# ScalarE's queue around the copy of a pair's second keys: attention, two MoE layers, one core

## The chip, the core and the metric

The kernel runs on one NeuronCore of a Trainium2 chip. The core's engines work side by side, each through a queue of its own in order: TensorE (PE: matrix products and transposes into PSUM; PEld is its weight load), VectorE (DVE), ScalarE (ACT), GpSimd (POOL) and SyncE (SP, which here issues DMAs). The metric is the device time of one execution in microseconds (us). The time before is 1155.35 us, the median of 3 runs (1152.71 to 1155.36).

## The reference

What is computed, cut to what matters (4 batches, 12 heads, 448 tokens, head size 64):

```
def _attn_ref(q, k, v, g_q, g_k):
    q_n, k_n = (rmsnorm(q, g_q), rmsnorm(k, g_k))
    scores = np.matmul(q_n, k_n.transpose(0, 1, 3, 2)) / np.sqrt(64)
    scores = scores - np.max(scores, axis=-1, keepdims=True)
    attn = np.exp(scores)
    return np.matmul(attn / (attn.sum(-1, keepdims=True) + 1e-09), v)
x = attention.transpose(0, 2, 1, 3).reshape(1792, 768)
h = np.maximum(x @ w_in, 0.0);  x = (h * h) @ w_out     # 768 -> 2048 -> 768
return (((x @ w1) * (x @ w2)) @ w3) @ moe2_w_out         # 768 -> 1024 -> 1024 -> 768
```

Products are made from a high and a low part of each operand (three matmuls for one product), so that every weight and every intermediate tile is split: a rounded copy (the high part) and the difference (the low part).

## The kernel before

The program is one loop over the 48 heads `h`, with one extra turn, and a generator of matmuls of the MoE layers that the loop draws on. `fill(n)` takes some n matmuls from it. While batch b's heads run (heads 12 to 23 are the second batch), the generator works on the MoE layers of an earlier batch: heads 0 to 12 have a product of weights (`gen_w3o`) beside them, 13 to 24 the MoE layers of the first batch (with the 64-bit weights that have to be turned into float32: `words` on ACT and POOL, `join` on DVE), 25 to 48 those of the second and part of the third. The rest follows behind the loop.

Heads go in pairs, an even one and the odd one behind it. The query rows of a pair are cut into seven chunks of 128: `CHUNKS` gives chunks 0 to 3 to the even head, 4 to 6 to the odd one, and chunk 3 holds the last 64 rows of both. So the scores of chunk 3, which the even head's turn makes, need the keys of the odd head. From head 12 on (`early`, line 1182) the keys of the next, odd head are therefore transposed in the even head's turn: `stage_k(h + 1)` (line 1185) issues four PE transposes (line 941) into the one PSUM bank `kv`, and ACT copies them to SBUF as the tile `kt` (line 943, shown as L144, the line of the helper). `stage_qk(h, 1)` behind it issues the scores (lines 956 and 957) of chunks 2 and 3; those of chunk 3 read the new `kt`. In this text "odd head 19" stands for the place in head 18's turn where the keys of head 19 are copied and used.

What stands in ACT's queue in such a turn, by the names in the rows: `vt` (copy out of the `kv` bank at the end of the head before), `vhl` (high part of v, `v_prep`), `nb` (line 988, scaling of the negated row maxima that DVE reduces in line 967), `p` (line 991, the exponentials), `ptr` and `pte` (high part of the transposed probabilities), `hl` (high part of a weight, `split_hi`), `raw` (lines 333 and 337, `words`), `r`, `act`, `acc`, `x`, `osb` (evictions of the MoE layers), `qn` and `nt` (statistics of the norm, every fourth head).

The order in each queue is not the order of the code. A scheduler takes what is ready first by its own estimate, and the code's order decides between equals. `issue_after(ins)` adds an edge without a semaphore: what is traced inside of it on `ins`'s engine stands behind `ins` in the queue. Before the change only `load` moves and the first heads use it. From the last half of the last batch's MoE layers on the order is the written one (`in_order`).

Of the kernel before, what the change touches and what calls it, by code (L numbers as in the profile page):

```python
# [8 lines left out]
F32 = mybir.dt.float32  # L9
# [21 lines left out]
def attention_moe_kernel(  # L31
# [18 lines left out]
    S = P * C  # L50
# [3 lines left out]
    NH = B * H  # L54
# [87 lines left out]
    def copy_on(eng, out, in_):  # L142
        if eng == "a":
            return nc.scalar.activation(out=out, in_=in_, func=AF.Copy)  # L144
        if eng == "g":
            return nc.gpsimd.tensor_scalar(out=out, in0=in_, scalar1=1.0, scalar2=1.0, op0=ALU.mult, op1=ALU.mult)
        return nc.vector.tensor_copy(out=out, in_=in_)
# [665 lines left out]
    def load_head(h):  # L813
        if not (0 <= h < NH):
            return
        b, hh = divmod(h, H)
        t = t2.tile([128, S], F32, name="qt", tag="qt")
        nc.sync.dma_start(out=t, in_=q_t[b, hh])
        qts[h] = t

    def load_v(h):
        if not (0 <= h < NH):
            return
        b, hh = divmod(h, H)
        t = t2.tile([128, C, D], F32, name="v", tag="v")
        nc.sync.dma_start(out=t, in_=v_in[b, hh])
        vs[h] = t
# [106 lines left out]
    def stage_k(h):  # L934
        if not (0 <= h < NH):
            return
        d = heads[h]
        khl = d.pop("khl")
        ps = ps_kv.tile([128, 512], F32R, name="kv", tag="kv")
        for c in range(C):  # L940
            nc.tensor.transpose(ps[:, c * P:(c + 1) * P], khl[:, c, :], ident_r[:P, :P])
        kt = t2.tile([128, S], F32R, name="kt", tag="kt")
        copy_on("a", kt, ps[:, :S].bitcast(F32))
        d["kt"] = kt

    def stage_qk(h, s):
        if not (0 <= h < NH):
            return
        d = heads[h]
        nb = d["nb"] = small.tile([128, 2], F32, name="nb", tag="nb")  # L950
        chunks = CHUNKS[h % 2][s]
        n = len(chunks)
        o = d["sc"] = [None] * n

        def score(out, d, at, m):
            nc.tensor.matmul(out, d["qh"][:, at:at + m], d["kt"], start=True, stop=False)  # L956
            nc.tensor.matmul(out, d["ql"][:, at:at + m], d["kt"], start=False, stop=True)  # L957

        for j, c in enumerate(chunks):
            ps = ps_sc.tile([128, 512], F32, name="sc", tag="sc")  # L960
            o[j] = ps[:, :S]
            if c == 3:
                score(o[j], heads[h + 1], S - 128, 128)
                score(o[j][:MIX], d, S - MIX, MIX)
            else:
                score(o[j], d, (c % 4) * 128, 128)
            nc.vector.tensor_reduce(out=nb[:, j:j + 1], in_=o[j], axis=AX.X, op=ALU.max, negate=True)  # L967
        if h < H:
            nc.vector.tensor_tensor(  # L969
                out=nb[:, :n], in0=nb[:, :n], in1=d["rq"][:, chunks[0]:chunks[0] + n], op=ALU.mult  # L970
            )
# [36 lines left out]
    def stage_words(h, s):  # L1008
        if not (H <= h < NH):
            return  # L1010
        d = heads[h]
        chunks = CHUNKS[h % 2][s]
        n = len(chunks)
        words = t3.tile([128, 2, S], F32R, name="pw", tag="pw")
        nc.sync.dma_start(out=words[:, :n].bitcast(F32), in_=d.pop("pp")[:, :n])
        for j, c in enumerate(chunks):
            d["p"][c] = words[:, j, :]

    def stage_sums(h):
        if 0 <= h < NH and h % 2:  # L1020
            flat, turned = sums2[h // 2]
            for b in range(0, 128, 32):
                nc.sync.dma_start(out=flat[:, b:b + 32], in_=turned[b:b + QC])
            sums2[h // 2] = flat
# [35 lines left out]
    def stage_lo(h):  # L1060
        if not (0 <= h < NH):
            return
        d = heads[h]
        for lo, p, hi in d["lo"]:
            sub_on("v", lo, p, hi)
        d["lo"] = []
# [51 lines left out]
    def fill(n):  # L1118
        state["credit"] += n
        while state["gen"] is not None and state["credit"] > 0:  # L1120
            try:
                k = next(state["gen"])
                state["credit"] -= k
                state["left"] -= k
            except StopIteration:
                state["gen"] = None
# [29 lines left out]
    for h in range(NH + 1):  # L1156
        n = W3O / ((H + 1) * 6) if h <= H else (MOE / (H * 6) if h <= 2 * H else (MOE + IN) / (2 * H * 6))
        late = h > 2 * H
        if h < 2:
            load_head(h + 3)  # L1160
            load_v(h + 1)
        if not late and h % GH == 0:
            load_group(h // GH + 1)
        stage_qk(h, 0)
        fill(n)
        if h <= 2 * H + 1:
            stage_sums(h - 1)
        stage_exp(h, 0)
        if h > 2 * H:
            stage_words(h, 0)  # L1170
        if h == 0:
            group_prep(0, "rest")
        if h >= 2:
            load_head(h + 3)
            load_v(h + 1)
        if late and h % GH == GH - 1:
            load_group((h + 1) // GH + 1)
        if h % H != 1:
            stage_x(h - 2)
        stage_t(h - 1, 0)  # L1180
        stage_t(h - 1, 1)
        early = H <= h and h % 2 == 0
        fill(n)
        if early:
            stage_k(h + 1)
        stage_lo(h - 1)
        if h < NH:
            v_prep(h)
        fill(n)
        if h <= 2 * H:  # L1190
            stage_words(h, 0)
        stage_rows(h - 1)
        even = H <= h
        if even:
            stage_qk(h, 1)
        if not early:
            stage_k(h + 1)
        stage_t(h - 1, 2)
        stage_t(h - 1, 3)
        fill(n)  # L1200
        stage_lo(h - 1)
        if not even:
            stage_qk(h, 1)
            fill(n)
        stage_exp(h, 1)
        if h > 2 * H:
            stage_words(h, 1)
        fill(n)
        if even:
            fill(n)  # L1210
        if h <= 2 * H:
            stage_words(h, 1)
        stage_v(h - 1)
        if h >= 2 * H and h % GH < 2:
            group_prep(h // GH + 1, "qk"[h % GH])
        elif h % GH == 1:
            group_prep(h // GH + 1)
        head_prep(h + 2)
        if h and h % H == 0:
            if h != 3 * H:  # L1220
                fill(1e9)
            stage_x(h - 1)
            if h == H:
                start_fill(gen_moe(0), MOE)
            elif h == 2 * H:
                in_order(SP)
                start_fill(gen_late(), MOE + IN)
            elif h == NH:
                start_fill(gen_pair(), MOE)
# [61 lines left out]
```

## Time and profile before

| | |
|---|---|
| time, median of 3 runs | 1155.35 us |
| profiled execution, its own time | 1159.42 us |
| span of the profile, first to last instruction | 1157.6 us |
| PE busy | 1124.8 us, 97% |
| DVE / ACT / POOL busy | 790.3 / 776.6 / 608.9 us |
| share of the chain that ended last | PE 67%, ACT 12%, DMA 7%, DVE 7% |

The profile's page gives the busy time of each engine, the span in 40 slices, the DMA queues, the chain of waits that ended last and the costliest groups of instructions. A name such as `sc<-kt` is a tile written and a tile read. A duration is that of one instruction; instructions of one engine overlap a little, so that the distance from start to start is shorter than the duration. Times are in us from the start of the span.

### The profile page before, as it was taken

The page shows a single profiled execution, that of the slowest core. Times are in us where ns is not written, and L with a number is a line of the kernel's source. Part 1 is how long each engine was busy: PE and PEld are TensorE (multiplying, and loading weights), DVE is VectorE, ACT ScalarE, POOL GpSimd, SP SyncE. Part 2 cuts the span into 40 slices and gives each one's busy share as a digit, 9 for nine tenths or more (in the row PEclk, how much of TensorE's full clock was granted, in tenths as well). Part 3 has the DMA queues.
Part 4 walks back from the last instruction along what each step waited for, and adds up shares of the span by engine and source line. Part 5 has one row for each costly group of instructions (what it writes and reads, how often), then busy time and mean ns, then how long its engine had stood idle before and what let it go on. Part 6 is the DMA issues. An engine that isn't in the chain of part 4 may idle for free.

```text
span 1157.6 us, 18785 instructions
## 1 busy us (share of the span) xinstructions
PE 1124.8 (97%) x5958; PEld 1019.5 (88%) x5958; DVE 790.3 (68%) x1363; ACT 776.6 (67%) x1768; POOL 608.9 (53%) x609
## 2 busy tenths in 40 slices
PE   7789999999999999999999999999999999999998
PEld 4678888999889899989989899999999899999997
DVE  6889888878898854565674755564544315887886
ACT  6889978888878866767776666776764435533352
POOL 3375433445545455957876776684865854011131
PEclk8899999999999999999999999999999999999999
DMA  7867757898998863565655657665556664243423
GB/s 237 264 201 211 235 160 243 306 297 293 321 294 276 279 190 120 165 213 178 219 172 163 207 182 236 197 197 165 171 170 202 215 193 126 69 135 105 130 83 123
DMA packets 130899, 229.74 MB, mean 198 GB/s; under 512 B 17472, under 2 KB 84544, under 8 KB 130800
## 3 DMA queue, kind: packets, MB, share of 16 engines
q1 hardware_dynamic: 129072, 225.79, 61.3%
q10 hardware_dynamic: 1728, 2.75, 0.7%
q8 instruction: 47, 0.77, 0.3%
q14 instruction: 52, 0.43, 0.1%
HBM read 162.53 MB, written 37.05 MB: 172 GB/s over the span
## 4 chain that ended last, share of the span: by engine, by line
PE 67%; ACT 12%; DMA 7%; DVE 7%; issue 3%; POOL 1%; SPq 1%; DVEq 0%; ACTq 0%; POOLq 0%
PE mm L411 16%; PE mm L412 16%; PE mm L413 16%; PE kv L1091 4%; PE pt L1045 3%; PE sc L956 2%; ACT p L991 2%; PE sc L957 2%; ACT raw L333 2%; ACT hl L144 2%; DMA raw<-wo 1%; DVE raw L346 1%; ACT ptr L144 1%; DMA raw<-w_in 1%; DMA raw<-w_out 1%
## 5 line engine op out<-in xcount | busy, mean ns | idle before, releaser
L150 POOL TENSOR_TENSOR hl<-raw,hl 128x384 fp32r<-128x384 f32 (+1 forms) x286 | 333.1, 1171 | 289.6 <-ACT hl L144 245.7
L144 ACT ACTIVATE hl<-raw 128x384 fp32r<-128x384 f32 (+1 forms) x405 | 227.8, 566 | 152.5 <-PE mm L413 40.1
L411 PE MATMUL mm<-x,hl 128*128 128x448 f32 (+1 forms) x640 | 238.3, 372 | 1.2 <-ACT x L144 1.2
L412 PE MATMUL mm<-x,hl 128*128 128x448 f32 (+1 forms) x640 | 234.2, 366 | 0.8 <-DVE x L150 0.8
L413 PE MATMUL mm<-x,hl 128*128 128x448 f32 (+1 forms) x640 | 233.7, 365 | 0.2 <-DVE hl L150 0.2
L411 PE MATMUL mm<-act,hl 128*128 128x448 f32 (+1 forms) x544 | 201.6, 371 | 1.9 <-ACT act L144 1.9
L412 PE MATMUL mm<-act,hl 128*128 128x448 f32 (+1 forms) x544 | 198.8, 365 | 3.7 <-DVE act L150 2.0
L413 PE MATMUL mm<-act,hl 128*128 128x448 f32 (+1 forms) x544 | 197.9, 364 | 0.1
L967 DVE TENSOR_REDUCE nb<-sc 128x1 f32<-128x448 f32 x168 | 102.6, 615 | 73.8 <-PE sc L957 72.4
L411 PEld LDWEIGHTS mm<-x,hl 128*128 128x128 f32 x640 | 121.0, 189 | 10.9 <-ACT x L144 2.3
L412 PEld LDWEIGHTS mm<-x,hl 128*128 128x128 f32 x640 | 121.0, 189 | 10.4 <-DVE x L150 1.8
L413 PEld LDWEIGHTS mm<-x,hl 128*128 128x128 f32 x640 | 120.9, 189 | 9.8 <-DVE hl L150 0.5
L991 ACT ACTIVATE p<-sc,nb,rr 128x448 f32<-128x448 f32 x168 | 121.3, 723 | 11.5 <-DVE nb L969 8.8
L150 DVE TENSOR_TENSOR ptr<-pt,ptr 128x512 fp32r<-128x512 f32 (+1 forms) x144 | 85.9, 617 | 57.9 <-ACT ptr L144 57.4
L412 PEld LDWEIGHTS mm<-act,hl 128*128 128x128 f32 x544 | 102.8, 189 | 12.3 <-DVE act L150 3.0
L411 PEld LDWEIGHTS mm<-act,hl 128*128 128x128 f32 x544 | 102.8, 189 | 9.5 <-ACT act L144 2.3
L413 PEld LDWEIGHTS mm<-act,hl 128*128 128x128 f32 x544 | 102.8, 189 | 8.0 <-DVE hl L150 0.4
L339 POOL TENSOR_SCALAR raw<-raw 128x384 uint32<-128x384 uint16 (+1 forms) x80 | 57.2, 716 | 83.1 <-DMA raw<-w_out 20.7
L346 DVE SCALAR_TENSOR_TENSOR raw<-raw 128x384 uint32<-128x384 uint32 (+1 forms) x120 | 86.4, 728 | 18.5 <-POOL raw L339 9.6
L956 PE MATMUL sc<-kt,qh 128*128 128x448 f32 (+1 forms) x192 | 74.8, 389 | 14.3 <-ACT p L991 7.4
L150 DVE TENSOR_TENSOR hl<-raw,hl 128x384 fp32r<-128x384 f32 (+1 forms) x119 | 80.0, 675 | 7.9 <-ACT hl L144 7.8
L333 ACT ACTIVATE raw<-raw 128x384 f32<-128x384 f32 (+1 forms) x120 | 71.6, 601 | 15.6 <-DMA raw<-w_in 7.7
(153 smaller groups left out, 2122.0 us busy)
## 6 DMA issues: line engine op xcount, KB each, us to landing
pw<-p SPq DMA_DIRECT2D x54, 448.0 KB
raw<-f_in SPq DMA_DIRECT2D x96, 192.0 KB
raw<-f_out SPq DMA_DIRECT2D x72, 256.0 KB
raw<-w_in SPq DMA_DIRECT2D x32, 384.0 KB
raw<-w_out SPq DMA_DIRECT2D x24, 512.0 KB
raw<-w SPq DMA_DIRECT2D x32, 384.0 KB
qt<-q_t SPq DMA_DIRECT2D x48, 224.0 KB
raw<-f SPq DMA_DIRECT2D x56, 192.0 KB
```

Of the source, the lines that this page charges most:

```text
L144: return nc.scalar.activation(out=out, in_=in_, func=AF.Copy)
L150: return (nc.vector if eng == "v" else nc.gpsimd).tensor_tensor(out=out, in0=in0, in1=in1, op=op)
L333: nc.scalar.activation(out=hi, in_=hi, func=AF.Prelu, scale=2.0**-112, alpha=-(2.0**32))
L339: nc.gpsimd.tensor_scalar(out=t[:, :n, 0], in0=low, scalar1=2.0**-13, scalar2=2.0**-14 - 0.5, op0=ALU.mult, op1=ALU.add)
L346: nc.vector.scalar_tensor_tensor(out=f[:, :n].bitcast(U32), in0=t[:, :n, 1], scalar=3, in1=t[:, :n, 0], op0=ALU.logical_shift_left, op1=AL ...
L411: nc.tensor.matmul(ps, w[:, 0, wk, :], x[0], start=(i == 0), stop=False)
L412: nc.tensor.matmul(ps, w[:, 0, wk, :], x[1], start=False, stop=False)
L413: nc.tensor.matmul(ps, w[:, 1, wk, :], x[0], start=False, stop=(i == last))
L956: nc.tensor.matmul(out, d["qh"][:, at:at + m], d["kt"], start=True, stop=False)
L967: nc.vector.tensor_reduce(out=nb[:, j:j + 1], in_=o[j], axis=AX.X, op=ALU.max, negate=True)
L991: nc.scalar.activation(out=p, in_=o[j], func=AF.Exp, scale=d["rq"][:, c:c + 1], bias=nb[:, j:j + 1], accum_out=sm[:, c:c + 1],)
L1091: nc.tensor.matmul(ps[:, :S], w, m, start=(n == 0), stop=(n == len(ops) - 1))
```

## The change

`stage_k` returns the instruction of the copy to `kt`. In the turns of even heads from 12 on, what is traced between `stage_k(h + 1)` and the end of the next `fill(n)` is placed behind that copy on ACT. In that stretch stand `stage_lo` (no work of ACT), `v_prep` (one copy on ACT) and the part of the MoE layers that `fill` draws (splits, words, evictions).

```
@@ -940,8 +940,8 @@
         kt = t2.tile([128, S], F32R, name="kt", tag="kt")
-        copy_on("a", kt, ps[:, :S].bitcast(F32))
         d["kt"] = kt
+        return copy_on("a", kt, ps[:, :S].bitcast(F32)).ins
@@ -1181,12 +1181,14 @@
         early = H <= h and h % 2 == 0
         fill(n)
-        if early:
-            stage_k(h + 1)
+        ahead = ExitStack()
+        if early and h + 1 < NH:
+            ahead.enter_context(tc.issue_after(stage_k(h + 1)))
         stage_lo(h - 1)
         if h < NH:
             v_prep(h)
         fill(n)
+        ahead.close()
```

No instruction is added or removed; the scheduler places them anew. From head 25 on, ACT's queue differs at each odd head by the copy `vhl`, which moves from well ahead of the copy `kt` to behind it. At odd head 37 (both pieces are of ACT's queue, the first in the turn's first third, the second at the copy):

```order
 L837 ACTIVATE nt<-nt 128x32
 L144 ACTIVATE vt<-kv 64x448
-L144 ACTIVATE vhl<-v 128x4x64
 L838 ACTIVATE nt<-nt 128x32
 L988 ACTIVATE nb<-nb,rr 128x1
...
 L144 ACTIVATE hl<-raw 128x384 x2
 L144 ACTIVATE kt<-kv 128x448
+L144 ACTIVATE vhl<-v 128x4x64
 L144 ACTIVATE act<-gf 128x448
 L144 ACTIVATE hl<-raw 128x384
```

Only `vhl` has moved; everything between the two pieces reads alike in both.

In the second batch more moves: words go behind `kt` too, and other instructions change places on ACT, DVE and POOL. At odd head 19 ACT's queue stood so before:

```order
L333 ACTIVATE raw_3814<-raw_3814 128x512
L144 ACTIVATE vt<-kv 64x448
L144 ACTIVATE vhl<-v 128x4x64
L483 ACTIVATE r<-mm 128x448
L144 ACTIVATE hl<-raw 128x512
L486 ACTIVATE act<-r 128x448
L988 ACTIVATE nb<-nb,rr 128x1 x2
L991 ACTIVATE p,sm<-sc,nb,rr 128x448 x2
L144 ACTIVATE ptr<-pt 128x384 x2
L144 ACTIVATE hl<-raw 128x512
L483 ACTIVATE r<-mm 128x448
L144 ACTIVATE kt<-kv 128x448
```

and from `nb` on it stands so now (`vt` is the row ahead of these, and `act`, `vhl` and `raw_3814` are the rows behind):

```order
L988 ACTIVATE nb<-nb,rr 128x1
L483 ACTIVATE r<-mm 128x448
L144 ACTIVATE hl<-raw 128x512
L486 ACTIVATE act<-r 128x448
L991 ACTIVATE p,sm<-sc,nb,rr 128x448
L988 ACTIVATE nb<-nb,rr 128x1
L144 ACTIVATE ptr<-pt 128x384
L991 ACTIVATE p,sm<-sc,nb,rr 128x448
L144 ACTIVATE ptr<-pt 128x384
L144 ACTIVATE hl<-raw 128x512
L483 ACTIVATE r<-mm 128x448
L144 ACTIVATE kt<-kv 128x448
```

The word `raw_3814` and `vhl` have left; the same eleven instructions stand ahead of `kt`, but the first `nb` now leads them. On DVE the join of `raw_3814`, which stood between the join of `raw_3743` and `xf`, has gone behind the low part of `vhl` as well.

At odd head 23, DVE's queue around the row maxima `nb` stood so before (`raw` rows are joins, `xf` the addition that empties the `kv` bank):

```order
L346 SCALAR_TENSOR_TENSOR raw<-raw_4888 128x384
L967 TENSOR_REDUCE nb<-sc 128x1
L1099 TENSOR_TENSOR xf<-kv,vt 64x448
L967 TENSOR_REDUCE nb<-sc 128x1
L542 TENSOR_TENSOR mm<-mm,r 128x448
```

and so now:

```order
L346 SCALAR_TENSOR_TENSOR raw<-raw_4869 128x384
L346 SCALAR_TENSOR_TENSOR raw<-raw_4888 128x384
L1099 TENSOR_TENSOR xf<-kv,vt 64x448
L967 TENSOR_REDUCE nb<-sc 128x1 x2
L542 TENSOR_TENSOR mm<-mm,r 128x448
```

The first reduction has moved behind `xf`; the joins ahead of it are the same.

## Rows read from the trace of the kernel before

**Rows 1.** Busy time by stretch; length, engines, PEclk, DMA share, GB/s

```profile
205.00:400.00 195.00, 191.01 (x1022) 173.96 (x1021) 170.44 (x292) 163.52 (x391) 95.88 (x103) 0.99 0.88 293
400.00:850.00 450.00, 446.72 (x2437) 408.54 (x2436) 255.84 (x414) 312.18 (x734) 308.93 (x292) 1.00 0.59 188
```

**Rows 2.** PE's waits, 205 to 850 us: total, times, longest

```profile
PE sc L956 <- ACT kt L144: 6.6, 6, 1.8
PE pt L1045 <- DVE ptr L150: 0.3, 1, 0.3
PE kv L941 <- DVE xf L1099: 0.2, 1, 0.2
```

**Rows 3.** PE timeline at odd heads 19 to 37: start, us, [idle before]

```profile
294.87 0.47 PE L956 MATMUL sc<-kt,qh 128*128 128x448 f32 x1 [1.51 <-ACT kt L144]
339.81 0.47 PE L956 MATMUL sc<-kt,qh 128*128 128x448 f32 x1 [0.35 <-ACT kt L144]
...
380.76 0.37 PE L957 MATMUL sc<-kt,ql 128*128 128x448 f32 x1
382.88 0.47 PE L956 MATMUL sc<-kt,qh 128*128 128x448 f32 x1 [1.75 <-ACT kt L144]
383.19 0.37 PE L957 MATMUL sc<-kt,ql 128*128 128x448 f32 x1
383.39 0.36 PE L956 MATMUL sc<-kt,qh 128*64 128x448 f32 x1
...
513.07 0.47 PE L956 MATMUL sc<-kt,qh 128*128 128x448 f32 x1 [1.48 <-ACT kt L144]
586.53 0.47 PE L956 MATMUL sc<-kt,qh 128*128 128x448 f32 x1 [0.92 <-ACT kt L144]
659.34 0.47 PE L956 MATMUL sc<-kt,qh 128*128 128x448 f32 x1 [0.58 <-ACT kt L144]
```

**Rows 4.** Busy time by stretch, 380 to 390 us (columns as in rows 1)

```profile
380.00:390.00 10.00, 8.25 (x37) 7.06 (x36) 8.50 (x16) 9.19 (x24) 4.73 (x6) 0.83 0.90 312
```

**Rows 5.** ACT timeline at odd heads 37 and 33

```profile
653.83 0.40 ACT L144 ACTIVATE vhl<-v 128x256 fp32r<-128x256 f32 x1
654.14 0.21 ACT L838 ACTIVATE nt<-nt 128x32 f32<-128x32 f32 x1
...
580.38 0.23 ACT L837 ACTIVATE nt<-nt 128x32 f32<-128x32 f32 x1 [2.69 <-DVE nt L836]
```

**Rows 6.** DVE and ACT timeline at odd head 29

```profile
507.52 0.62 DVE L967 TENSOR_REDUCE nb<-sc 128x1 f32<-128x448 f32 x1
...
507.85 0.40 ACT L144 ACTIVATE vhl<-v 128x256 fp32r<-128x256 f32 x1
508.18 0.29 ACT L988 ACTIVATE nb<-nb,rr 128x1 f32<-128x1 f32 x1
```

**Rows 7.** ACT timeline at odd head 21

```profile
333.70 0.29 ACT L988 ACTIVATE nb<-nb,rr 128x1 f32<-128x1 f32 x1 [0.62 <-DVE nb L967]
...
339.21 0.54 ACT L144 ACTIVATE kt<-kv 128x448 fp32r<-128x448 f32 x1
```

**Rows 8.** DVE, then ACT timeline at odd head 19

```profile
288.65 0.69 DVE L346 SCALAR_TENSOR_TENSOR raw<-raw 128x512 uint32<-128x512 uint32 x1 [0.54 <-POOL raw L339]
289.79 1.14 DVE L967 TENSOR_REDUCE nb<-sc 128x1 f32<-128x448 f32 x2
...
289.14 0.54 ACT L483 ACTIVATE r<-mm 128x448 f32<-128x448 f32 x1
294.25 0.56 ACT L144 ACTIVATE kt<-kv 128x448 fp32r<-128x448 f32 x1
```

**Rows 9.** ACT timeline at odd head 23

```profile
376.63 0.29 ACT L988 ACTIVATE nb<-nb,rr 128x1 f32<-128x1 f32 x1 [1.88 <-DVE nb L967]
381.82 0.57 ACT L333 ACTIVATE raw<-raw 128x384 f32<-128x384 f32 x1
382.26 0.56 ACT L144 ACTIVATE kt<-kv 128x448 fp32r<-128x448 f32 x1
```

More of the change, by code (lines that the diff above doesn't have):

```diff
@@ L942, in stage_k @@
         kt = t2.tile([128, S], F32R, name="kt", tag="kt")
-        copy_on("a", kt, ps[:, :S].bitcast(F32))
         d["kt"] = kt
+        return copy_on("a", kt, ps[:, :S].bitcast(F32)).ins
     def stage_qk(h, s):
@@ L1183, in attention_moe_kernel @@
         fill(n)
-        if early:
-            stage_k(h + 1)
+        ahead = ExitStack()
+        if early and h + 1 < NH:
+            ahead.enter_context(tc.issue_after(stage_k(h + 1)))
         stage_lo(h - 1)
@@ L1189, in attention_moe_kernel @@
         fill(n)
+        ahead.close()
         if h <= 2 * H:
```

## The prediction

> **What bounds the kernel now.** I read the busy times by stretch first, because the change acts only between the first odd head it touches and the end of the loop. There the reader sees a PE that is busy for 191.0 of 195 us and 446.7 of 450 us, at a granted clock of 0.99 and 1.00 of full speed, while ACT is busy for 163.5 and 312.2 us [rows 1]. PE sets the time; another engine matters only where PE waits for it. Who that is, the view of waits says: between 205 and 850 us PE sits idle for 6.6 us, in six places, for the copy `kt`, and for 0.5 us for anything else; it waits for no weight, no eviction and no transfer [rows 2]. The timeline of PE then shows the six places: the odd heads 19, 21, 23, 29, 33 and 37, with 1.51, 0.35, 1.75, 1.48, 0.92 and 0.58 us of idle time [rows 3]. The twelve other odd heads that the change touches lose almost nothing.
>
> A place costs a little more than its idle time. At head 23 the scores start at 380.76, then at 382.88 and, one matmul later, at 383.19 [rows 3]. Undisturbed, such matmuls follow each other every 0.20 us (383.19 to 383.39). So 2.12 + 0.31 - 0.40 = 2.03 us are lost for 1.75 us of idle time, 0.28 more. With 0.28 for each of the six the waits cost 6.6 + 1.7 = 8.3 us.
>
> Behind the longest wait the clock falls: between 380 and 390 us the mean granted clock is 0.83 of full speed [rows 4], which is 10 x 0.17 / 0.5 = 3.4 us at the lower of the two levels, 1.2 GHz. Work in it takes twice as long, so 1.7 us are lost. No other wait of rows 3 has that behind it: the stretch from 400 to 850 us, with three of them, has a clock of 1.00 [rows 1]. Together 10.0 us is all that this change can win at `kt`, 0.9% of the time.
>
> **What the change takes away, from head 25 on.** The copy `kt` is late because ACT has a backlog: at head 23 it starts at 382.26 straight behind a word that started at 381.82, with no pause between them [rows 9]. What can make it earlier is what leaves the queue ahead of it. From head 25 on that is `vhl` alone, one copy of 0.40 us, 12 times (front part, first order rows). Three of these places have a wait.
> - Head 37: `vhl` starts at 653.83 and the next instruction at 654.14, so 0.31 us leave [rows 5]. ACT works without a pause from there to `kt`. The wait of 0.58 us becomes 0.27.
> - Head 33: behind `vhl` ACT sits idle for 2.69 us until 580.38, for the statistics on DVE [rows 5]. What leaves ahead of that only makes the pause longer: nothing is won, 0.92 us stay.
> - Head 29: `nb` starts at 508.18, right behind `vhl`. But it also needs DVE's reduction, which runs from 507.52 for 0.62 us, to 508.14 [rows 6]. Without `vhl` it starts at the same moment: nothing is won, 1.48 us stay.
>
> **What it does in the second batch** (heads 13 to 23). Here words leave as well, but other instructions change places, so I count ACT's queue from `nb` to `kt` anew.
> - Head 21: from `nb` at 333.70 to `kt` at 339.21 are 5.51 us [rows 7]. Three words leave, of 0.44 us each (as at head 23, 381.82 to 382.26 [rows 9]). One other word, one weight split and one short `nt` come in between, 0.44 + 0.5 + 0.2 as I estimate from the distances around them. That is 5.51 - 1.32 + 1.14 = 5.3 us. `nb` itself can come earlier, since the maxima now stand ahead of the norm's statistics on DVE. So `kt` starts by 339.0 at the latest, ends 0.54 us later, and the wait of 0.35 us shrinks to 0.1 or goes; I take it as gone, with its surcharge 0.6 us.
> - Head 19: before, `r` starts at 289.14 and `kt` at 294.25; eleven instructions in 5.11 us [rows 8]. The same eleven stand there now, but led by `nb`, which waits for DVE. On DVE the join at 288.65 leaves (0.69 us and 0.54 us of waiting ahead of it), so that the first reduction starts about 1.2 us before 289.79, at 288.6, and ends 0.6 us later [rows 6, 8]. 289.2 + 5.1 = 294.3: `kt` is where it was, and 1.5 us of idle time stay. What was won at the words is lost because `r`, `hl` and `act`, which ran while DVE was at work, now stand behind `nb`.
> - Head 23: from `nb` at 376.63 to `kt` at 382.26 are 5.63 us [rows 9]. The word at 381.82 (0.44 us) leaves and another comes; a split of about 0.5 us moves ahead of `nb`. That makes about 5.1 us. But `nb` now comes later: DVE's first reduction stands behind `xf`, one instruction of about 0.5 us. The two cancel, and 1.75 us and the fall of the clock stay.
> - Heads 13, 15 and 17 have no wait to lose. I take 0 for them; the third case below prices the other side.
>
> **What is moved behind.** `vhl` is read at the end of the next turn, and the words that move are taken up three units ahead of use; DVE's and POOL's parts of them stand later in their queues too, so they do not block. That PE waits for no weight and no `vhl` now [rows 2] says there is cover; 0 is my value. If the cover failed, each of the twelve words that move could cost its own 0.57 us [rows 9] at the weight that it feeds: 6.8 us is the other end, and only a slower DVE or transfer chain could bring a part of it.
>
> **The sum.** 0.31 + 0.6 = 0.9 us off the profiled execution: 1159.42 - 0.9 = 1158.5 us. That execution ran 4.07 us over the median of the runs (1155.35), and the waits should be in both; so I forecast 1155.35 - 0.9 = 1154.4 us. This is under 0.3% (3.5 us), which is about what a measurement of this kernel can tell from no change.
>
> **The rivals.**
> - *The waits of the second batch go.* For it speaks that words of 0.44 us leave at every one of its places, and that at head 19 ACT could start the eleven instructions at once behind `vt` if DVE came earlier by more than the 1.2 us I count. Against it: at 19 and 23 my count puts `kt` where it was. Price: at 19 1.51 + 0.28, at 23 1.75 + 0.28, and the 1.7 us of the clock with it, on top of 0.9: 6.4 us, 1149.0 us. If 29 and 33 went too, 3.0 us more; but nothing leaves the queue there that binds.
> - *The clock alone.* The Trainium skill, page "TensorE: Matmul & The Clock Gate", section "What's actually happening", says that a gate sets the array's clock by how busy the engine has been of late. By that rule a shorter wait at head 23 would give back the slow stretch too. The trace bears it out as far as the fall follows the longest wait, and does not settle it, since 1.51 and 1.48 us had none behind them. In rows: a wait that shrinks at 23 from 1.75 to 1.4 us wins 0.35 + 1.7, on top of 0.9: 1152.4 us. I count this with the first half of the range.
> - *`nb` ahead of work that was ready makes `kt` later* (slower). In the second batch the scheduler now puts `nb`, which waits for DVE, in front of `r`, `hl` and `act`. If DVE's first reduction at head 19 is not earlier than before, it ends at 290.4, and `kt` starts at 290.4 + 5.1 = 295.5, 1.25 us later. It decides from the point where that reduction ends after 289.15. Were it so at 19 and 23, and at two of 13, 15 and 17 for about 0.8 us each, it is 2.5 + 1.6 = 4.1 us, and each wait that grows past 1.75 us may bring 1.7 us of slow clock, taken once: 5.8 us less the 0.9 won, 1160.2 us. For it speaks the order at 19; against it that the joins ahead of the maxima on DVE get fewer.
> - *The change does not do what it says.* From head 25 on it nearly does not: the splits and evictions ahead of `kt` were traced ahead of it and stay. This is in my forecast.
>
> **How the numbers follow.** The forecast 0.52 (its own range 1152.5 to 1156.5), the first rival 0.14, the clock 0.12, the slower one 0.17, and 0.05 for a gain at 29 and 33 beside those. The first rival and the last lie below 1151.9 us (0.3%), and a fifth of the clock's and the forecast's spread reaches there too: faster 0.23. The slower rival lies half beyond 1158.8 us as it stands or with a second fall of the clock, and some spread comes on top: slower 0.14. The rest, 0.63, is within 0.3%. The range that holds 8 in 10 takes in the first rival, from 1148.8, and ends short of the slower one's full price, at 1158.8; a gain at 29 and 33 and the failed cover are left out.
>
> **What would show it.** In the changed kernel's view of PE's waits for `kt` between 205 and 850 us: the idle time of six places should fall from 6.6 to about 5.9 us, with head 37 near 0.27 us, 29 and 33 at 1.5 and 0.9, 21 gone, 19 and 23 near 1.5 and 1.75. No wait of PE for weights or `vhl` should appear. I am wrong if 19 and 23 are gone or if a wait stands at 13, 15 or 17; if the waits are as I say and the time still moves by over 3 us, the clock or the part behind 850 us did it.

## The result, and the profile after

The changed kernel takes 1159.14 us (median of 15 runs), the kernel before 1154.41 us in the same comparison (15 runs): a ratio of 1.0065, 95% interval 1.0049 to 1.0081. This ratio is the comparison's estimate over all runs of both kernels; the quotient of the two medians is 1.0041 (4.7 us), that of the means 1.0059. The forecast was 1154.4 us and no measurable change; the kernel became slower, by an amount just past the end of the range.

| | before | after |
|---|---|---|
| profiled execution, its own time, us | 1159.42 | 1163.71 |
| TensorE busy, 205 to 400 us | 191.01 | 187.56 |
| TensorE busy, 400 to 850 us | 446.72 | 446.96 |
| its waits for `kt`, 205 to 850 us | 6.6 us, 6 times | 5.6 us, 4 times |
| its waits for the transfer `pw` there | under 0.2 us | 2.9 us, 3 times |

The first view to read is again the busy time by stretch, with the columns of [rows 1]; here of the changed kernel:

```profile
205.00:400.00 195.00, 187.56 (x998) 170.90 (x996) 169.87 (x288) 159.32 (x376) 89.07 (x98) 0.99 0.87 286
400.00:850.00 450.00, 446.96 (x2444) 409.83 (x2445) 264.73 (x418) 315.65 (x742) 310.01 (x293) 1.00 0.60 190
```

Against [rows 1], TensorE loses 3.45 us of busy time and 24 matmuls in the second batch, and gains 0.24 us behind it. The loss is in the part where the forecast expected a gain of 0.6. TensorE's waits in the changed kernel, 205 to 850 us (total, times, longest):

```profile
PE sc L956 <- ACT kt L144: 5.6, 4, 2.4
PE pt L1045 <- DMA pw<-p: 2.9, 3, 2.1
PE pt L1045 <- DVE ptr L150: 1.2, 2, 0.6
PE kv L941 <- DVE xf L1099: 0.4, 1, 0.4
```

The waits for `kt` fall by 1.0 us against [rows 2], as meant. What is new is the second line: the transposes of the probabilities wait for `pw`, the transfer on SP's queue that turns the exponentials `p` into the tile the transposes read. Two of its three places (the third wait is 0.3 us, at 400 us) and those of `kt`, on TensorE's timeline (start, duration, idle before); at 361.83, between them, the transposes wait for DVE's low part `ptr`:

```profile
221.80 0.71 PE L1045 MATMUL pt<-ident_r,pw 128*128 128x128 f32 x6 [0.53 <-DMA pw<-p]
...
294.43 0.47 PE L956 MATMUL sc<-kt,qh 128*128 128x448 f32 x1 [2.37 <-ACT kt L144]
...
361.83 0.37 PE L1045 MATMUL pt<-ident_r,pw 128*128 128x128 f32 x2 [0.59 <-DVE ptr L150]
...
375.32 0.28 PE L1045 MATMUL pt<-ident_r,pw 128*128 128x128 f32 x2
377.73 0.45 PE L1045 MATMUL pt<-ident_r,pw 128*128 128x128 f32 x3 [2.13 <-DMA pw<-p]
...
385.71 0.47 PE L956 MATMUL sc<-kt,qh 128*128 128x448 f32 x1 [1.14 <-ACT kt L144]
...
515.18 0.47 PE L956 MATMUL sc<-kt,qh 128*128 128x448 f32 x1 [1.53 <-ACT kt L144]
587.83 0.47 PE L956 MATMUL sc<-kt,qh 128*128 128x448 f32 x1 [0.52 <-ACT kt L144]
```

Against [rows 3]: heads 21 and 37 have no wait left, 29 is unchanged, 19 has grown from 1.51 to 2.37 us, and a wait of 2.13 us stands at 377.73, where there was none. The clock falls once, as before, but now behind head 19 instead of head 23 (compare [rows 4]):

```profile
290.00:300.00 10.00, 7.55 (x33) 6.15 (x32) 7.79 (x15) 10.00 (x25) 5.47 (x6) 0.83 0.88 272
380.00:390.00 10.00, 8.86 (x50) 7.76 (x49) 7.16 (x15) 9.47 (x25) 4.05 (x5) 1.00 0.96 292
```

**Why `pw` is late at 377.73.** SP's queue of the changed kernel (SPq rows: start, time to issue, line; L319 loads a raw weight, L354 stores a joined one):

```profile
356.26 0.50 SPq L354 DMA_DIRECT2D f<-raw  x1
363.04 0.33 SPq L319 DMA_DIRECT2D raw<-w  x1
363.41 0.43 SPq L354 DMA_DIRECT2D f<-raw  x1
363.94 0.49 SPq L1015 DMA_DIRECT2D pw<-p  x1
...
369.03 0.94 SPq L354 DMA_DIRECT2D f<-raw  x1
372.31 0.33 SPq L319 DMA_DIRECT2D raw<-w  x1
372.69 0.42 SPq L354 DMA_DIRECT2D f<-raw  x1
373.21 0.47 SPq L1015 DMA_DIRECT2D pw<-p  x1
```

SP stands still from 356.8 to 363.0 and from 370.0 to 372.3, each time at a load, and `pw` is issued behind it: the second one at 373.21, against 366.67 before, and TensorE asks for it at 375.60. The load waits for a buffer, which a join on DVE sets free:

```profile
SPq L319 <- DVE raw L346: 12.7, 7, 5.4
```

This is SP's wait for joins between 335 and 375 us; it was 7.3 us in all, 4.1 the longest, before. The join itself ends at 363.01, just ahead of the load at 363.04; ACT's timeline at its word, and DVE's at the join:

```profile
361.41 0.57 ACT L333 ACTIVATE raw<-raw 128x384 f32<-128x384 f32 x1
361.85 0.58 ACT L337 ACTIVATE raw<-raw 128x384 uint32<-128x384 uint16 x1
...
361.08 1.29 DVE L150 TENSOR_TENSOR ptr<-pt,ptr 128x512 fp32r<-128x512 f32 x2 [0.57 <-ACT ptr L144]
362.45 0.56 DVE L346 SCALAR_TENSOR_TENSOR raw<-raw 128x384 uint32<-128x384 uint32 x1
```

The join now stands behind two low parts and starts when the second piece of its word has ended (362.43), because this word (`raw_4650`) was moved from between the exponentials to behind the copies `ptr` on ACT: 361.41 instead of 354.68, 6.7 us later, where its neighbours are about 2.2 us later. SP's own order at this place is the same in both kernels.

**The two profiled executions.** Their times differ by 4.3 us, but not by these waits alone. Taking the same matmul in both traces: the changed kernel is 2.2 us ahead at 170 us, 1.7 behind at 432, 0.3 behind at 849, and 4.3 behind at the end. The last 4 us are the last 220 us of the program, where no wait differs; experiment 7 is on that.

### The profile page after: what moved, and what is told of

It is laid out like the page before. It is cut to its first block, busy times and chain, and to the rows that moved or that the text cites. A ratio compares the mean times of both kernels' runs of the same rounds, so it can differ in the third digit from the quotient of the medians.

```text
span 1161.9 us, 18791 instructions
## 1 busy us (share of the span) xinstructions
PE 1124.4 (97%) x5958; PEld 1016.9 (88%) x5958; DVE 801.8 (69%) x1363; ACT 778.1 (67%) x1768; POOL 606.1 (52%) x609
## 4 chain that ended last, share of the span: by engine, by line
PE 63%; DVE 11%; ACT 11%; DMA 8%; issue 5%; POOL 2%; SPq 1%; DVEq 0%; ACTq 0%; POOLq 0%
PE mm L411 15%; PE mm L412 15%; PE mm L413 15%; PE kv L1091 3%; DVE raw L346 3%; PE pt L1045 2%; ACT p L991 2%; PE sc L956 2%; PE sc L957 2%; ACT raw L333 2%; DMA raw<-wo 1%; ACT hl L144 1%; ACT ptr L144 1%; DVE nb L967 1%; PE sc L413 1%
## 5 line engine op out<-in xcount | busy, mean ns | idle before, releaser
L150 POOL TENSOR_TENSOR hl<-raw,hl 128x384 fp32r<-128x384 f32 (+1 forms) x286 | 331.7, 1166 | 302.3 <-ACT hl L144 259.4
```

The lines of the kernel that those rows point to most:

```text
L150: return (nc.vector if eng == "v" else nc.gpsimd).tensor_tensor(out=out, in0=in0, in1=in1, op=op)
```

## The experiments

Theory 1: the loss is made in the second batch, by what the new order does to ACT, DVE and SP there. Theory 2: it is made behind 850 us. All edits are of the kernel before or the changed one; ratios are to the kernel before on the same chip, with 95% intervals. "Idle" is TensorE's idle time between 165 and 430 us in the profile (265 less its busy time), the last column SP's longest wait for a join between 335 and 375 us.

| | kernel | ratio | interval | idle, us | SP, us |
|---|---|---|---|---|---|
| | before (profile) | 1 | | 4.4 | 4.1 |
| | after | 1.0065 | 1.0049 to 1.0081 | 8.5 | 5.4 |
| 1 | edges from head 24 on | 1.0001 | 0.9982 to 1.0019 | 4.2 | 4.0 |
| 2 | edges 12 to 22 | 1.0043 | 1.0025 to 1.0060 | 7.8 | 5.9 |
| 3 | `vhl` alone behind `kt` | 1.0067 | 1.0043 to 1.0091 | 6.7 | 4.9 |
| 4 | after, `pw` written earlier | 1.0040 | 1.0020 to 1.0059 | 8.5 | 5.2 |
| 5 | edges from head 18 on | 1.0037 | 1.0016 to 1.0057 | 6.2 | 4.0 |
| 6 | edges 12, 14, 16 | 1.0052 | 1.0032 to 1.0071 | 8.5 | 6.1 |
| 7 | after once more | 1.0059 | 1.0033 to 1.0086 | 8.4 | 6.1 |
| 8 | before, late `kt` on DVE | 1.0012 | 0.9989 to 1.0035 | 3.9 | 4.0 |
| 9 | before, one word late | 0.9982 | 0.9965 to 0.9999 | 3.1 | 4.2 |
| 10 | after, that word early | 1.0031 | 1.0016 to 1.0047 | 5.1 | 3.5 |
| 11 | after, `nb` behind `act` at 19 | 1.0058 | 1.0036 to 1.0079 | 7.6 | 6.1 |
| 12 | 1 and 9 together | 1.0004 | 0.9984 to 1.0025 | 3.3 | 4.2 |
| 13 | 10 and 11 together | 1.0055 | 1.0033 to 1.0076 | 6.5 | 3.5 |
| 14 | edge 12 alone | 1.0029 | 1.0012 to 1.0046 | 7.7 | 5.3 |
| 15 | edge 14 alone | 1.0006 | 0.9988 to 1.0024 | 5.6 | 3.3 |
| 16 | edge 16 alone | 1.0038 | 1.0020 to 1.0055 | 6.8 | 5.5 |

Kernels 1, 2, 5, 6 and 14 to 16 differ from the changed one by a condition on the edge:

```
-        if early and h + 1 < NH:
-            ahead.enter_context(tc.issue_after(stage_k(h + 1)))
+        if early:
+            kt_ins = stage_k(h + 1)
+            if 2 * H <= h and h + 1 < NH:    # 1; 2: h < 2 * H; 5: h >= 18 and h + 1 < NH;
+                ahead.enter_context(tc.issue_after(kt_ins))    # 6: h <= 16; 14 to 16: h == 12, 14, 16
```

**1. The edges of the third batch and later alone.**

> The edge behind the copy `kt` is kept only from the third batch on (even heads 24 and later); the second batch has the order of before. Theory 1 (the loss is made in the second batch, by what its new order does to the queues of ACT, DVE and SP): the loss is gone, and what remains is the gain of heads 29 to 37, 0.3 to 1 us: ratio to before 0.999 to 1.000, about 1153.8 us against 1154.4. TensorE is at 400 us within 0.6 us of where before has it. Theory 2 (the second batch costs little; the last 240 us run in the slower rhythm of 206.7 ns per matmul in the changed kernel, because the change shifts how TensorE starts again at 920 us): the order behind 400 us is that of the changed kernel, so the slow rhythm of the last part should appear here as well, ratio 1.003 to 1.006.

Theory 1 holds. Idle at head 37 is gone, 29 stands at 1.48 and 33 at 1.03 us. That would be the term of 0.3 us that the prediction had for this part, but it is too small to show in the ratio, and kernels 6 and 9, with the order of before behind head 25, have no wait at 37 either. The slow rhythm of the last part was not there. TensorE's place was missed: by head 25 it is 5.7 us ahead of the kernel before, 3.3 of it before head 12, all in the same order.

**2. The edges of the second batch alone.**

> The edge behind the copy `kt` is kept only in the second batch (even heads 12 to 22); from head 24 on the order is that of before. Theory 1 (the second batch's new order): as slow as the changed kernel or a little slower, ratio to before 1.004 to 1.008, about 1160 us, and of it 3.5 to 4 us between 165 and 400 us. Theory 2 (rhythm of the last part, by the order behind 400 us): 1.000 to 1.003. In both the waits for `kt` at heads 29, 33 and 37 are those of before (0.85 to 1.8 us lost at each).

Theory 1 holds here too: TensorE waits for `pw` four times, 2.5 us in all, between 165 and 400 us. Up to head 24 all queues have the order of the changed kernel, and still the waits for `kt` at heads 21 and 23 are exchanged: 1.13 us at 21 and none at 23 here, none and 1.14 there.

```profile
338.87 0.47 PE L956 MATMUL sc<-kt,qh 128*128 128x448 f32 x1 [1.13 <-ACT kt L144]
```

So which of these two places waits differs from one execution to the next.

**3. `vhl` alone behind `kt`**, the words left free:

```
         if h < NH:
             v_prep(h)
-        fill(n)
         ahead.close()
+        fill(n)
```

> Only the copy `vhl` is queued behind `kt`; what the MoE generator draws behind the transposes is left free. If the loss comes from the moved words (they come later on ACT, so joins, stores and, behind them on SP, the transfer `pw` come later), it is mostly gone: ratio to before 0.999 to 1.003, and TensorE's wait for `pw` in the second batch is under 0.7 us. If it comes from the other moves of the second batch (the scheduler places everything anew once one copy moves), it stays: 1.004 to 1.008, with waits for `kt` or `pw` of 2 us or more in place of those of before.

The loss stays, in another shape: almost no wait for `pw` (0.2 us), but seven waits for `kt`, 7.6 us in all between 205 and 850 us, one of them at head 15, which had none, and 1.89 us at head 21. So it isn't the words held behind `kt` as such; moving one copy of 0.4 us makes the scheduler place the batch anew, and this order is as bad.

**4. The changed kernel, `pw` written ahead of the transposes** in even heads 12 to 24:

```
+        if h <= 2 * H and early:
+            stage_words(h, 0)
         fill(n)
         ahead = ExitStack()
...
-        if h <= 2 * H:
+        if h <= 2 * H and not early:
             stage_words(h, 0)
```

> The changed kernel with one more edit: in even heads 12 to 24 the transfer of the first half of the probabilities (`pw`) is written in the code ahead of the transposes, so that in SP's queue it stands two pairs of load and store earlier. If the wait for `pw` is what the second batch lost (0.66 us at 221.8, 0.77 at 361.8, 2.1 at 377.7, about 3 us with surcharges, by the profile of the changed kernel), the ratio to before falls from 1.0065 to 1.003 to 1.004 and no wait of TensorE for `pw` is left between 205 and 400 us. If the `pw` wait only stands in for another wait that ends a little earlier (the row maxima or `kt` on ACT), the ratio stays at 1.005 to 1.008 and `kt` waits grow by 1.5 us or more. If the loss is the slower rhythm of the last 240 us, it stays too, with that rhythm in the trace.

Inconclusive. The ratio came to the expected 1.004, with an interval that overlaps the changed kernel's. But the waits for `pw` did not go (3.0 us in three), since the second half of `pw`, which is late at 377, had not been moved.

**5 and 6. The edges split by whether `kt` is late there.** An edge at 18, 20 or 22 alone leaves SP's queue as it is and moves only rows around itself; one at 12, 14 or 16 changes SP's queue over many heads. This gave theories A and B.

> The edge behind `kt` only from even head 18 on (odd heads 19, 21, 23 and all later ones). In this form SP's queue keeps the order of before, and the other queues change at each edge's own place only. Theory A (the loss is a knock-on of the edges at heads 12, 14 and 16, where `kt` was not waited for: they re-plan words, joins and transfers as far as head 23): most of the loss is gone, ratio to before 0.999 to 1.002; what stays is `kt` at head 19, idle for 2.3 to 2.4 us in place of 1.5, and no wait of TensorE for `pw` over 0.5 us between 355 and 400 us. Theory B (the loss is made by the edges at the places where `kt` is late, 19 to 23): as slow as the changed kernel, 1.004 to 1.007, with the waits for `pw`.

> The edge behind `kt` only at even heads 12, 14 and 16. Theory A (knock-on): slow, ratio to before 1.003 to 1.006, with waits of TensorE for `pw` near 362 and 377 us of 0.7 us and about 2 us, and SP waiting for a join for over 5 us near 360 us, as in the changed kernel; `kt` at head 19 idle for 1.5 to 1.9 us as before. Theory B (the edges at 18, 20, 22): 0.999 to 1.002, no such waits.

A holds for kernel 6: the three edges at places that had no wait to lose make nearly the whole loss alone. TensorE's timeline in kernel 6 at heads 19 and 22:

```profile
294.93 0.47 PE L956 MATMUL sc<-kt,qh 128*128 128x448 f32 x1 [2.36 <-ACT kt L144]
...
377.60 0.54 PE L1045 MATMUL pt<-ident_r,pw 128*128 128x128 f32 x4 [2.07 <-DMA pw<-p]
```

These are the changed kernel's two waits, without any edge at 18, 20 or 22. (Near 362 us it has none; in the changed kernel the wait there is for `ptr`, not for `pw`, as the expectations had it.) Against A, `kt` at 19 isn't the local edge's doing: it is 2.36 here and 1.07 in kernel 5. And kernel 5 wasn't free: 1.0037, with `kt` at 21 (1.30), where the edge was to help, and a wait of 0.68 us for `pw` at 308 us. With kernel 1 (1.0001) in mind that is a cost of the edges at 18 to 22, at the places where `kt` is late. The parts don't add up: 0.37 and 0.52% apart, 0.6% together.

**7. The changed kernel once more.**

> The changed kernel, nothing edited, profiled once more. If the slower rhythm of its last 220 us (206.7 ns from matmul to matmul instead of 202.7, some 4 us in all) belongs to that one execution, this profile has 202.7 there, as the five other profiles have; the waits of the second batch are there again: `kt` at head 19 idle for 2.3 to 2.4 us, `pw` near 377 us for about 2 us. If the rhythm belongs to the changed kernel, it is there again. Ratio to before 1.005 to 1.007 in both cases.

Both as expected by the first reading. `kt` at 19 is idle for 2.36 us and `pw` near 380 us for 1.89. The rhythm of the last part, busy time 920 to 1140 us of the first profile and of this one:

```profile
920.00:1140.00 220.00, 220.00 (x1065) 199.84 (x1066) 142.26 (x238) 94.58 (x184) 62.70 (x56) 1.00 0.40 121
```

```profile
920.00:1140.00 220.00, 219.78 (x1085) 203.39 (x1084) 147.10 (x243) 96.11 (x186) 64.14 (x57) 1.00 0.41 125
```

The same program, at a granted clock of 1.00 both times, gets 1065 or 1085 matmuls done in 220 us. So theory 2 falls as the cause; that part of the 4.3 us between the first two profiles was chance.

**8. `kt` on DVE behind the second batch**, in the kernel before:

```
-        copy_on("a", kt, ps[:, :S].bitcast(F32))
+        copy_on("v" if h > 2 * H else "a", kt, ps[:, :S].bitcast(F32))
```

> The kernel before, with the copy `kt` on DVE instead of ACT for all heads behind the second batch. ACT is busy for 312 of 450 us there and DVE for 256. If the waits for `kt` at heads 29, 33 and 37 (1.48, 0.92 and 0.58 us idle, 3.8 us with surcharges) are ACT's backlog alone, they go, and the ratio to before is 0.997 to 0.999. If what stands ahead of `kt` on DVE is as long (the reductions of the maxima, the low parts), or the scheduler's new order makes waits elsewhere as in the second batch, it is 0.999 to 1.003.

No gain to be measured. Two waits of 2.0 us in all, 1.45 of it at head 29, replace the three of 3.0. At head 29 DVE sits idle for 2.10 us until ACT has copied `ptr`, makes its low parts and only then copies `kt` (506.48 to 507.10); the scores follow at 507.24.

**9. One word late, in the kernel before.** This puts `raw_4650` where the changed kernel has it, without any other edge (the line that makes `stage_t` return the copy is left out):

```
-        stage_t(h - 1, 1)
+        t_ins = stage_t(h - 1, 1)    # the copy to ptr, returned by stage_t
         early = H <= h and h % 2 == 0
-        fill(n)
+        with tc.issue_after(t_ins) if h == 21 else ExitStack():
+            fill(n)
```

> The kernel before with one edge of its own: in the turn of head 21 what the generator draws in the third unit of the turn is queued on ACT behind the copy `ptr`. By that one word (`raw_4650`) stands eight places later on ACT, and its join stands behind the low parts of `ptr` on DVE, as the edges at heads 12 to 16 have it; nothing else changes but the rows around it. Theory A (one word that comes late holds its buffer, SP waits at the load that wants the buffer, and the transfer `pw` behind it on SP comes late): SP waits for joins for 10 us or more between 335 and 375 us in place of 7 to 8, TensorE waits for `pw` near 377 us for 1 to 2 us, ratio to before 1.001 to 1.003. Rival (the queues have slack enough for one word; the waits come only when ACT as a whole has fallen behind): no such wait, ratio 0.998 to 1.001.

Theory A's size was wrong and its rival right: not slower (0.9982), and no wait at this place. SP and TensorE there (two rows of each):

```profile
365.17 0.42 SPq L354 DMA_DIRECT2D f<-raw  x1
365.69 0.47 SPq L1015 DMA_DIRECT2D pw<-p  x1
...
369.00 0.36 PE L413 MATMUL mm<-x,hl 128*128 128x448 f32 x1
369.21 0.82 PE L1045 MATMUL pt<-ident_r,pw 128*128 128x128 f32 x6
```

`pw` is issued 3.5 us ahead of its use and is in time. In the kernel before it was 7.5 us (366.67 to 374.20), in the changed one 2.1 (373.21 to 375.32), and TensorE waited 2.13. All 18 profiles agree on this transfer: TensorE doesn't wait for it in the nine with a lead of 3.4 us or more, and waits 0.2 to 2.1 us in the nine with 3.2 or less. So the cover was 4.1 us in the profile of before, and 2.8 in that of kernel 1, which has the same order here and a lead of 6.2. One late word takes most of it (3.5 us against 6.2 and 7.5). What takes the rest in the changed kernel, where ACT's neighbours of the word are late too, isn't shown by itself.

**10. That word early, in the changed kernel** (`turn["h"]` is the head of the turn; the lines that set it are left out):

```
-            upto("word", i + WORD_AHEAD, lambda k: is64(k) and words(k))
+            upto("word", i + WORD_AHEAD + (20 <= turn["h"] <= 21), lambda k: is64(k) and words(k))
```

> The changed kernel with words drawn one unit earlier in the turns of heads 20 and 21: the word that had moved behind the copies `ptr` stands between the exponentials again, and SP's queue is the same in every row. Theory A: SP's wait for joins between 335 and 375 us falls from 13 to 8 to 10 us, TensorE's waits for `pw` near 362 and 377 us (2.7 to 3 us with surcharges) go or fall below 1 us in all, ratio to before 1.003 to 1.004 in place of 1.006. Rival (ACT as a whole is behind): the waits stay or turn into a longer wait for `kt` at heads 21 and 23, ratio 1.005 to 1.007.

Theory A here: by the ratio half of the loss comes back (kernel 13, with the same edit and another, doesn't repeat it), and the waits for `pw` fall from 2.9 to 0.3 us (205 to 850 us). Its detail on SP was wrong: the sum of the waits for joins stays (13.8), only the longest falls, from 5.4 to 3.5. It is the long one that a `pw` stands behind.

**11. `nb` behind ready work at head 19, in the changed kernel** (the lines that keep the last `act` copy are left out):

```
-        stage_exp(h, 0)
+        with tc.issue_after(act_last[0]) if h == 18 else ExitStack():    # the last `act` copy
+            stage_exp(h, 0)
```

> The changed kernel with one exchange on ACT at odd head 19: `r`, `hl` and `act` stand ahead of the first `nb` again, as in the kernel before; no other row of any engine moves. Theory C (the third rival of the prediction, at head 19: `nb` waits for DVE's reduction, and work that was ready waits behind it): those three, 1.4 us by their starts, run in the 3.3 us that ACT sat idle ahead of `nb`, so `kt` starts 1.2 to 1.4 us earlier against TensorE, the wait at head 19 falls from 2.36 to 1.0 to 1.2 us idle, and no fall of the clock follows it (1.7 us more): ratio to before 1.003 to 1.005 in place of 1.006. Rival (`kt` is late there because DVE's joins, not the order on ACT, hold what stands ahead of it): the wait stays over 2 us and the ratio at 1.005 to 1.007.

DVE, then ACT at head 19 in the changed kernel, and ACT in this one:

```profile
285.81 1.88 DVE L346 SCALAR_TENSOR_TENSOR raw<-raw 128x512 uint32<-128x512 uint32 x3
287.61 0.61 DVE L1099 TENSOR_TENSOR xf<-kv,vt 64x448 f32<-64x448 f32 x1
288.14 1.14 DVE L967 TENSOR_REDUCE nb<-sc 128x1 f32<-128x448 f32 x2
...
288.78 0.30 ACT L988 ACTIVATE nb<-nb,rr 128x1 f32<-128x1 f32 x1 [3.34 <-DVE nb L967]
289.10 0.55 ACT L483 ACTIVATE r<-mm 128x448 f32<-128x448 f32 x1
...
293.81 0.57 ACT L144 ACTIVATE kt<-kv 128x448 fp32r<-128x448 f32 x1
```

```profile
285.45 0.55 ACT L484 ACTIVATE r<-mm 128x448 f32<-128x448 f32 x1
285.89 0.63 ACT L144 ACTIVATE hl<-raw 128x512 fp32r<-128x512 f32 x1
286.41 0.57 ACT L487 ACTIVATE act<-r 128x448 fp32r<-128x448 f32 x1
288.64 0.29 ACT L989 ACTIVATE nb<-nb,rr 128x1 f32<-128x1 f32 x1 [1.66 <-DVE nb L968]
...
292.47 0.56 ACT L144 ACTIVATE kt<-kv 128x448 fp32r<-128x448 f32 x1
```

The mechanism is as theory C has it: `r`, `hl` and `act` were ready, and run in the pause; `kt` starts 1.3 us earlier, with `vt` at the same time in both, the wait falls from 2.37 to 1.51 us (1.0 to 1.2 expected), the clock doesn't fall there. But the ratio is what it was, and the profile shows where most of the gain went:

```profile
339.53 0.47 PE L957 MATMUL sc<-kt,qh 128*128 128x448 f32 x1 [0.88 <-ACT kt L144]
...
384.75 0.47 PE L957 MATMUL sc<-kt,qh 128*128 128x448 f32 x1 [1.95 <-ACT kt L144]
```

Heads 21 and 23 together take 2.83 us, where the three profiles with the changed kernel's order (kernels 2 and 7 too) take 1.06 to 1.14, and the clock falls at 380 to 390 us instead. Kernel 13 repeats this against kernel 10: 0.85 us less at head 19, 0.83 more at 21 and 23. Against it the wait for `pw` near 376 us falls to 1.07 us, so that TensorE's idle time is 7.6 us and not 8.5: too little for the ratio to show. I read a wait of TensorE as time in which ACT, DVE and SP catch up, so that one taken away comes back at the next places; that it is this, and not their order, is not shown.

**12. Late edges and the late word together.**

> The kernel before with the two edits that cost nothing or won something alone: the one word of head 21's turn behind the copies `ptr`, and the edge behind `kt` from head 24 on. If the 0.18% that the word alone won (interval 0.01 to 0.35%) is there, and the late edges bring their 0.3 to 1 us: ratio to before 0.997 to 0.999. If that gain was chance: 0.999 to 1.001.

The gain of kernel 9 was not found again. No version here is shown to beat the kernel before.

**13. Both local exchanges in the changed kernel.**

> The changed kernel with both local exchanges: words one unit earlier in the turns of heads 20 and 21, and `r`, `hl`, `act` ahead of `nb` at odd head 19. If these two places are the loss, and the second one's gain is lost only because the late word makes waits behind it: ratio to before 0.999 to 1.002, TensorE idle for under 5 us between 165 and 430 us (4.4 in the kernel before, 8.5 in the changed one). If ACT and DVE as a whole are behind, so that a wait taken away in one place comes back in the next: 1.002 to 1.004, no better than the words alone.

The second case, though above its range (1.0055): no better than the word alone (the intervals of 10 and 13 overlap). The two places that I had found are not the sum of the loss.

**14 to 16. One early edge each.**

> The kernel before with the edge behind `kt` at head 12 alone. If one of the three early edges makes the loss, one of these three runs is at 1.004 to 1.006 and two are within 0.999 to 1.001. If any new placing costs, all three are at 1.002 to 1.005.

> The kernel before with the edge behind `kt` at head 14 alone; expectations as for the edge at head 12 alone.

> The kernel before with the edge behind `kt` at head 16 alone; expectations as for the edge at head 12 alone.

Neither case: two of three cost 0.3 to 0.4%, one nothing. Each gives the second batch another order, with its waits at other places (at head 23 `kt` is 2.40 us late with the edge at 12, and not at all with the one at 14).

## Why the prediction was wrong

- *"Heads 13, 15 and 17 have no wait to lose. I take 0 for them."* This is the step that failed. Their edges alone make 0.52% (kernel 6). I had counted an edge at the place where it stands, and it is a new order for the batch: words, joins and SP's transfers move as far as head 23, where the code is untouched. The other side that the prediction kept for them was a longer `kt` at these heads; it came at 19 and at `pw`. The same step fails for the edges at 18, 20 and 22, which I had counted as a gain of 0.6 us: the edges from 18 on cost 0.37% by themselves (kernel 5).
- *"What is moved behind: 0 is my value."* The consumers I named never waited: no wait for a weight or for `vhl` appears. The moved words hold something else, the buffer of a load, and SP's queue stands at that load with `pw` behind it. I said that DVE's and POOL's parts do not block, and named a slower transfer chain without looking at SP's queue. Price: 2.9 us in three waits, within the 6.8 us of the other end.
- *Head 19: "`kt` is where it was."* It is 0.86 us later. The condition of the third rival came true: against TensorE DVE's first reduction was not 1.2 us earlier but where it was (0.13 us ahead of the transposes of the keys, at 288.27 now and 289.92 before), since three joins and `xf` stand ahead of it, as many as before, and `r`, `hl` and `act` waited behind `nb` for it. Kernel 11 shows this by one exchange on ACT. The rival's price for the place was 1.25 us. In kernel 5 `nb` leads these three too, but there the reduction starts 1.9 us ahead of the transposes, and the wait is 1.07 us. That the order at 19 comes from the early edges (kernel 6) and not from its own, I had not seen.
- *Head 23: "1.75 us and the fall of the clock stay."* 1.14 us, 1.06 in kernel 7 and none in kernel 2, which has the same order there, and the fall moved to head 19 (behind `pw` in kernel 2). So a shorter wait at 23 came true, the condition of the rival on the clock, but the slow stretch was not given back. Why the wait is shorter is not shown: without the wait for `pw` ahead of it (kernel 10) it is 1.17.
- Right: 29 unchanged, and nearly nothing from head 25 on (kernel 1: 1.0001). Heads 21 and 37 have no wait, where none and 0.27 us were forecast, but that is luck as far as the runs show: kernel 2 waits 1.13 us at 21 in the changed kernel's order, kernels 1 and 8 have none there in the order of before, and kernels 6 and 9 none at 37 without an edge. So the two terms of the sum, 0.31 and 0.6 us, rested on waits of one execution. Head 33 was forecast unchanged at 0.92; it was 0.52 after, 0.36 in kernel 7 and 1.03 in kernel 1, which has the same order of DVE and PE there.
- The third rival's time, 1160.2 us, was the nearest, with half of its mechanism. I left its full price outside the range because I looked for it at waits for `kt` alone.

The size: idle time of TensorE in the second batch grows from 4.2 us (mean of the profiles of before and of kernels 1 and 8, which have the same order there) to 8.5 (both profiles of the changed kernel). With 0.28 us for each of some five more waits and less 0.4 us won behind 430 us that is 5.3 us, 0.46%. The fall of the clock (1.7 us) was in both profiles of the changed kernel and in one of those three: 1.1 us more. A direct reading of the second batch is near that: from the transposes of head 12's keys to those of head 25's, TensorE takes 262.4, 260.0 and 259.4 us in those three profiles, 266.6 and 267.1 in the two of the changed kernel, 6.3 more. The measured 0.65% is 7.5 us, its lower end 5.7; the medians differ by 4.7. What fills the rest, if there is one, stays open. Also open is which of the moved instructions make the half of the loss that kernel 10 doesn't give back.

## What to carry to other kernels

Where a scheduler places the work, an ordering edge is priced by the whole difference of the order, on every queue, SP's too, and not at its own line. Edges only where the waits are were no way out here (kernel 5). An in-order queue that holds both loads waiting for buffers and a transfer that TensorE needs passes a delay of the loads on to the transfer, and to TensorE once the transfer's lead is used up, so measure that lead (here 6.2 to 7.5 us, of which 3.2 to 3.4 were needed) before moving what frees the buffers. A wait removed in a stretch where the feeding engines are nearly full (ACT and DVE 84 and 87% of 205 to 400 us) can come back at the next two places: look there for it. And before a forecast is built on a wait of half a microsecond, look whether a second execution has it.

## What the runs showed of the hardware

- *Two rhythms at full clock.* In 6 of 18 profiles (among them the first of the changed kernel, not its second) TensorE does 921 or 922 matmuls from 940 to 1130 us, in the other 12 it does 939 or 940, with TensorE busy for all of the 190 us: about 206.7 or 202.7 ns from start to start, some 4 us by the end. Whether the new order brings the slow one more often, and so makes part of what stays open above, is not shown: it is in one of the five profiles with the second batch's order of before or one word moved (before, 1, 8, 9, 12), and in five of the other 13. A single profile of this kernel can mislead by that much.
- *The clock falls at some waits of a size and not at others.* Nine of the 18 profiles have one stretch of slow clock (1.2 GHz) between 160 and 850 us, each inside or right behind a wait of 1.75 to 2.4 us. But six more waits of that size have none: 2.35 us at head 19 in kernel 4, 1.88 at head 23 in kernel 1, 2.36 at head 19 in kernels 2 and 6, and the waits for `pw` in both profiles of the changed kernel, 2.13 and 1.89. The Trainium skill, page "TensorE: Matmul & The Clock Gate", section "What's actually happening", ties the clock to how busy the engine has been of late; every fall seen here comes with a wait, which agrees, and what tells the waits with a fall from those without, no run here shows.
